# Block-sparse attention and a softplus FFN on one core: attention handed out in two pieces per unit instead of three, and TensorE in the program's own order

## The chip, the core and the metric

The kernel runs on one core of a Trainium2 chip. A core has five engines that work at the same time, each through its own queue in order: TensorE (PE; its weight loads are listed apart as PEld), VectorE (DVE), ScalarE (ACT), GpSimd (POOL) and SyncE (SP, which only issues DMAs here). The metric is the device time of one execution in microseconds (us). Matmul results land in PSUM, in eight banks; DMAs move data between HBM and the on-chip memory SBUF.

## The reference

Four batches of eight heads, 768 positions of 64 channels. A query block of 32 positions sees its neighbours, the first and the last block, and three sampled blocks; the first and the last query block see everything. The result, 3072 tokens of 512 channels, goes through one FFN with a softplus between its two matrices.

```python
scores = scale * np.matmul(q, k.transpose(0, 1, 3, 2))
mask = np.abs(blk_i - blk_j) <= window
mask = mask | (blk_i == 0) | (blk_j == 0) | (blk_i == n_blocks - 1) | (blk_j == n_blocks - 1)
for qb in range(n_blocks):
    for kb in sampled_blocks[qb]:
        mask[qb * block:(qb + 1) * block, kb * block:(kb + 1) * block] = True
...
attn = attn / (np.sum(attn, axis=-1, keepdims=True) + 1e-09)
x = np.matmul(attn, v)                      # then (tokens, heads * channels)
h = x @ w_in
g = np.maximum(h, 0.0) + np.log1p(np.exp(-np.abs(h)))
return g @ w_out
```

The weights come in 64 bit and are converted on the core; FFN operands are split into a high and a low part, so that each product takes three matmuls (high with high, high with low, low with high).

## The kernel before

**Attention.** A *set* is one group of four query blocks of a batch with all eight heads; each batch has six groups (the last with two blocks) and one *whole* set, the first and last query block against all 24 key blocks. That makes 28 sets. Each set has two *units* (a = 0 and 1, four heads each). A unit n goes through these steps, named by the tile that they write:

- `scores` (L581): 16 small matmuls into two PSUM tiles `s` (L601; `nc.tensor.matmul` on f32 stands twice in the trace, so 32 there), then VectorE's scaled and masked minimum, four instructions, out of `s` into `pr` (L607), which frees the `s` tiles. Whole sets: L625 and L632, four `s` tiles.
- `exponents` (L642): ScalarE, four activations on `pr` (L657).
- `transposes` (L661): eight TensorE transposes (L670) of `pr` into two PSUM tiles `t`, copied to `pt` by ScalarE (L677) and VectorE (L675).
- `values` (L682): 32 small matmuls (L700; 64 in the trace) of `pt` with the values `vg` into the PSUM tile `x` of the set, of which there is one buffer; whole sets L714.

When a set's two units are through, `normalise` divides (VectorE, L728 to L730, into `xs`), `turn` transposes `xs` on TensorE (L745, tile `y`), and `x_high` (ScalarE, L759) and `x_low` (VectorE, L763) write the two parts of the FFN's input `x`.

The tiles `s`, `t`, `y` and the FFN's hidden tile `h` all share four PSUM buffers (tag "s" of `ps_s`). A tile that takes a buffer must wait until the tile before it there was read.

**What feeds it.** Query, key, value and weight loads are issued by SyncE in the order of the program. Keys of a batch lie in one buffer `kT`; `gather_keys` copies the blocks of a set into `kg` (two buffers; sampled blocks by GpSimd, L511, ends by ScalarE, L480, the window by VectorE, L497). Values have two buffers `vg`: `load_values(m + 2)`, issued after the values matmuls of set m, brings the window and the ends, and GpSimd gathers the sampled blocks (L567). `gather()` (L460) takes one such GpSimd job of values and one of keys each time it is called. The next batch's keys are loaded after the scores of the whole set's second unit.

**FFN.** 128 steps of 384 tokens by 128 hidden columns, in two phases (48 and 80 steps). A step has 12 hidden matmuls (L237 to L239) and nine of the projection into three PSUM tiles `o` (L295 to L297), with softplus on ScalarE and VectorE between (L243 to L273). The weights of the first phase are converted while attention runs (`Weights.tick`, called through `convert`).

**Order.** `pieces(n)` (L768) makes three functions per unit: a score piece (`x_low`, then scores of unit n + 2, keys), a value piece (exponents of n + 2, `turn`, values of n, loads of values and queries) and a transpose piece (`x_high`, `normalise`, transposes of n + 1). `attend` (L862) runs the next piece, one `gather()` and one `convert()`. The first 22 pieces run alone; then the FFN starts, and `between(x)` (L898), called in the middle of the hidden matmuls, between the projection's three parts and at the half and end of a step, runs as many pieces as are due at that point: `due` (L888) spreads them evenly over the steps of the next 384 tokens. With three pieces per unit and about one step per unit, TensorE sees, over and over: scores, six hidden, three projections, values, six projections, transposes, six hidden.

SyncE's queue is in the order of the program. The other engines' queues, TensorE's among them, were ordered by the scheduler at build time, which in most places of TensorE's queue left the order of the program.

Of the kernel before, what the change touches and what calls it, by code (L numbers as in the profile page):

```python
# [32 lines left out]

FIRST = 11

START = 4

SPREAD = 2

# [11 lines left out]
def sparse_attention_ffn(  # L51
# [408 lines left out]
    def gather():  # L460
        for work in (value_work, key_work):
            if work:
                work.pop(0)[1]()
# [178 lines left out]
    def exponents(n):  # L642
        m, a = units[n]
        b, g, whole = sets[m]
        st = state[n]
        if a == 0:

            sums[m] = wk.tile([P, 2 * NP], F32, tag="sums", name=f"sums{n}", bufs=3)
        rs, nmax, rows = sums[m], st["nmax"], slice(0, st["rows"])
        for r in range(2):  # L650
            if whole:
                parts = [(st["pr"][r], 0, 2 * a + r)]
            else:
                w = NS * BLOCK
                parts = [(st["pr"][r][rows, j * w : (j + 1) * w], j, 2 * (2 * a + j) + r) for j in range(2)]
            for x, j, h in parts:
                nc.scalar.activation(  # L657
                    x, x, AF.Exp, bias=nmax[rows, r, j : j + 1], scale=-1.0, accum_out=rs[rows, h : h + 1]
                )
# [21 lines left out]

    def values(n):  # L682
        m, a = units[n]
        b, g, whole = sets[m]
        pt = state[n]["pt"]
        gathered(value_work, m)
        vd = vg[sets[m]]
        if a == 0:
            xps[m] = ps_x.tile([P, DM], F32, tag="x", name=f"x{n}")
        xq = xps[m]  # L690

        if not whole:
            ni = NI if g < NG - 1 else 2
            for j in range(2):
                for r in range(2):
                    h = 2 * (2 * a + j) + r
                    for c in range(2):
                        for i in range(ni):
                            rows = slice(i * BLOCK, (i + 1) * BLOCK)
                            nc.tensor.matmul(  # L700
                                xq[rows, h * D : (h + 1) * D],
                                pt[r, 2 * j + c][:, rows],
                                vd[:, c, i, h * D : (h + 1) * D],
                                start=(c == 0), stop=(c == 1),
                            )
        else:
            rows_v = vd.rearrange("p c i f -> p (c i) f")
            for r in range(2):
                at = (2 * a + r) * D
                for c in range(NCH):  # L710
                    for o in range(2):
                        rows = slice(64 * o, 64 * o + 64)
                        h = 2 * (2 * a + o) + r
                        nc.tensor.matmul(  # L714
                            xq[rows, at : at + D],
                            pt[r, c][:, rows],
                            rows_v[:, c, h * D : (h + 1) * D],
                            start=(c == 0), stop=(c == NCH - 1),
                        )
# [18 lines left out]
    def turn(m):  # L738

        b, g, whole = sets[m]  # L740
        xs = xss.pop(m)
        rows = P if whole or g < NG - 1 else 2 * BLOCK
        ps = ps_s.tile([P, NP, P], F32, tag="s", name=f"y{m}")
        for p in range(NA if whole else NP):
            nc.tensor.transpose(ps[:, p, 0:rows], xs[0:rows, p * P : (p + 1) * P], ident[0:rows, 0:rows])  # L745
        t, at = divmod(place[b, g], GROUPS)
        if (0, t) not in X:
            x_tile(0, t)
        if whole:
            hi, lo = (X[0, t][:, i, :, at * P + 64 : (at + 1) * P] for i in range(2))  # L750
            src = ps[:, 0:NA].rearrange("p a (o t) -> p (a o) t", o=2)
        else:
            hi, lo = (X[0, t][:, i, :, at * P : at * P + rows] for i in range(2))
            src = ps[:, :, 0:rows]
        turned[m] = (hi, lo, src)

    def x_high(m):
        hi, lo, src = turned[m]
        nc.scalar.copy(out=hi, in_=src)  # L759
# [8 lines left out]
    def pieces(n):  # L768

        ended = [units[i][0] if 0 <= i < len(units) and units[i][1] == NA - 1 else None for i in range(n - 2, n + 1)]  # L770

        scored = None
        if n + 2 < len(units) and units[n + 2][1] == NA - 1 and not sets[units[n + 2][0]][2]:
            scored = place[sets[units[n + 2][0]][:2]]

        def score_piece():
            if ended[0] is not None:
                x_low(ended[0])
            s = n + 2
            if s < len(units):  # L780
                scores(s)
                if scored is not None:
                    load_keys(scored + 2)
                m, a = units[s]
                b, g, whole = sets[m]
                if whole and a == NA - 1 and b + 1 < B:

                    gathered(key_work, place[b, g])
                    for n_ in range(4):
                        load_kT(b + 1, n_)  # L790
                    load_keys()

        def value_piece():
            if n + 2 < len(units):
                exponents(n + 2)
            if ended[1] is not None:
                turn(ended[1])
            if n < len(units):
                values(n)
                if ended[2] is not None:  # L800
                    load_values(ended[2] + 2)
            if scored is not None:
                load_queries(scored + 2)

        def transpose_piece():
            if ended[1] is not None:
                x_high(ended[1])
            if ended[2] is not None:
                normalise(ended[2])
            if n + 1 < len(units):  # L810
                transposes(n + 1)

        return score_piece, value_piece, transpose_piece

# [38 lines left out]
    spread_ends()  # L855
    attention = [piece for n in range(len(units) + 2) for piece in pieces(n)]

    needs = [3 * sum(1 for m, a in units if place[sets[m][:2]] < (t + 1) * GROUPS) + 4 for t in range(NTB)]
    needs[-1] = len(attention)
    done = 0  # L860

    def attend():  # L862
        nonlocal done
        attention[done]()
        done += 1
        gather()
        convert()

    SECOND = NTB * EARLY
    owed = 0.0  # L870

    def convert():

        nonlocal owed
        if done < START:
            return
        owed += EARLY_TICKS if weights.at < 4 * len(early) + 9 else LATE_TICKS
        while owed >= 1 and not weights.done():
            weights.tick()
            owed -= 1  # L880
            if weights.at == 4 * weights.extra + 2:
                extractx.close()
                pools["x2"] = ctx.enter_context(tc.tile_pool(name="x2", bufs=1))
# [97 lines left out]
```

## Time and profile before

| What | us |
|---|---|
| Median of three runs | 831.7 |
| Lowest and highest of the three | 827.58 and 833.89 |
| Span of the profiled execution, first to last instruction | 812.1 |
| TensorE busy in the span | 781.7 |
| VectorE, ScalarE, GpSimd busy | 574.8, 489.6, 223.3 |

The profile gives the span of the profiled execution, not its device time; the median of the runs is 19.6 us longer than that span.

A row of the timeline has start (us from the span's start), duration, engine, line, operation, tiles, shape and count; in brackets stands the time that the engine was idle before it and what ended that ("issue" when the profile shows nothing that it waited for). Matmuls overlap: what one costs on TensorE is the distance between two starts, not its duration. A row of the windows view has a stretch, its length, and for each engine the busy time in it with the number of instructions.

### The profile page before, as it was taken

Reading aid. Unit: us, or ns where it says so; the run is one execution under the profiler, and the core shown is the slowest. Engines: PE = TensorE matmul, PEld = TensorE weight load, DVE = VectorE, ACT = ScalarE, POOL = GpSimd, SP = SyncE. Lnnn points to the kernel's source line nnn. Section 1 sums busy time; section 2 is a strip of 40 time slices with the busy share of each in tenths; the row PEclk is TensorE's granted clock in tenths of the full one; section 3 lists DMA queues with packets and bytes.
Section 4 is the critical chain, followed back from the end, with each engine's and each line's share of the span. In section 5 each row is a group of like instructions: output and inputs, shape, how many; then the busy total and the mean of one; then the engine's idle time right before and its main releaser. Section 6 shows DMA issues by size and latency. Waiting matters only on the chain.

```text
span 812.1 us, 21433 instructions
## 1 busy us (share of the span) xinstructions
PE 781.7 (96%) x8108; PEld 647.6 (80%) x8108; DVE 574.8 (71%) x1474; ACT 489.6 (60%) x1182; POOL 223.3 (27%) x389
## 2 busy tenths in 40 slices
PE   8878898999999999999999999999999999999997
PEld 8545676877677777778778988999988999988996
DVE  5778999876887777886655985656565656656564
ACT  5878785757767767767565764444444444444442
POOL 6864775635565436563000000000000000000000
PEclk9999898999999999999999999999999999999999
DMA  8899678687696777866425640304040312122021
GB/s 254 241 257 336 171 212 266 195 294 247 184 291 198 248 261 200 267 171 184 158 78 182 250 178 20 137 1 155 2 146 10 116 40 105 52 88 68 0 79 40
DMA packets 48408, 129.65 MB, mean 160 GB/s; under 512 B 5489, under 2 KB 5617, under 8 KB 46257
## 3 DMA queue, kind: packets, MB, share of 16 engines
q1 hardware_dynamic: 42304, 109.79, 42.3%
q0 software_dynamic: 5712, 17.57, 7.6%
q8 instruction: 64, 1.05, 0.5%
q10 hardware_dynamic: 288, 0.93, 0.3%
q14 instruction: 40, 0.32, 0.1%
HBM read 97.85 MB, written 30.41 MB: 158 GB/s over the span
## 4 chain that ended last, share of the span: by engine, by line
PE 82%; DVE 7%; ACT 6%; DMA 2%; issue 2%; POOL 0%; SPq 0%; ACTq 0%; DVEq 0%; POOLq 0%
PE o L295 11%; PE h L237 11%; PE o L297 10%; PE o L296 10%; PE h L238 10%; PE h L239 10%; PE s L601 5%; PE t L670 4%; PE x L700 4%; ACT pr L657 3%; PE warm L831 2%; DMA kT<-in_k_dram 1%; PE s L625 1%; DVE pr L607 1%; PE x L714 1%
## 5 line engine op out<-in xcount | busy, mean ns | idle before, releaser
L237 PE MATMUL h<-x,w 128*128 128x384 f32 x512 | 180.0, 352 | 0.4 <-DVE nmax L632 0.2
L238 PE MATMUL h<-x,w 128*128 128x384 f32 x512 | 173.7, 339 | 0.0
L239 PE MATMUL h<-x,w 128*128 128x384 f32 x512 | 173.1, 338 | 0.0
L250 DVE TENSOR_SCALAR u<-e 128x384 f32<-128x384 f32 x128 | 50.8, 397 | 155.8 <-ACT e L244 154.4
L295 PE MATMUL o<-w,gh 128*128 128x512 f32 x384 | 158.7, 413 | 0.0
L657 ACT ACTIVATE pr<-pr,nmax 128x256 f32<-128x256 f32 (+2 forms) x208 | 110.4, 532 | 74.6 <-DVE nmax L607 60.4
L297 PE MATMUL o<-w,gl 128*128 128x512 f32 x384 | 152.0, 396 | 1.2 <-issue 1.0
L296 PE MATMUL o<-w,gh 128*128 128x512 f32 x384 | 151.7, 395 | 0.0
L243 ACT ACTIVATE e<-h 128x384 f32<-128x384 f32 x128 | 62.4, 487 | 114.9 <-PE h L239 114.8
L267 ACT CAST gh<-u 128x384 fp32r<-128x384 f32 x128 | 65.6, 513 | 79.2 <-PE o L296 78.1
L237 PEld LDWEIGHTS h<-x,w 128*128 128x128 f32 x512 | 96.6, 189 | 19.4 <-issue 11.2
L567 POOL DMA_INDIRECT vg<-in_v_dram,ix x88 | 90.3, 1027 | 65.9 <-PE x L700 39.1
L238 PEld LDWEIGHTS h<-x,w 128*128 128x128 f32 x512 | 96.8, 189 | 6.5 <-issue 2.2
L511 POOL COPY kg<-kT 128x128 f32 x252 | 86.0, 389 | 41.2 <-PE s L601 38.8
L239 PEld LDWEIGHTS h<-x,w 128*128 128x128 f32 x512 | 96.6, 189 | 0.0
L295 PEld LDWEIGHTS o<-w,gh 128*128 128x128 f32 x384 | 72.0, 188 | 19.9 <-issue 7.1
L297 PEld LDWEIGHTS o<-w,gl 128*128 128x128 f32 x384 | 72.1, 188 | 18.8 <-issue 1.5
L296 PEld LDWEIGHTS o<-w,gh 128*128 128x128 f32 x384 | 72.2, 188 | 10.3 <-issue 0.4
L607 DVE CUSTOM_DVE_ANT_1 pr<-s,mask 128x256 f32<-128x256 f32 (+1 forms) x192 | 69.6, 414 | 14.5 <-PE s L601 14.5
L258 ACT ACTIVATE u<-u 128x384 f32<-128x384 f32 x128 | 66.9, 523 | 15.4 <-DVE e L252 15.2
L263 DVE TENSOR_TENSOR u<-u,e 128x384 f32<-128x384 f32 x128 | 73.6, 575 | 3.0 <-ACT u L258 2.4
L273 DVE TENSOR_TENSOR gl<-u,gh 128x384 fp32r<-128x384 f32 x128 | 73.0, 570 | 2.8 <-ACT gh L267 2.8
(81 smaller groups left out, 1088.6 us busy)
## 6 DMA issues: line engine op xcount, KB each, us to landing
vg<-in_v_dram SPq DMA_DIRECT2D x19, 768.0 KB, 5.8
xD<-x SPq DMA_DIRECT2D x8, 1536.0 KB, 7.4
x<-xD SPq DMA_DIRECT2D x8, 1536.0 KB
raw<-in_w_in_dram SPq DMA_DIRECT2D x16, 512.0 KB, 9.3
raw<-in_w_out_dram SPq DMA_DIRECT2D x16, 512.0 KB, 8.3
qc<-in_q_dram SPq DMA_DIRECT2D x24, 256.0 KB, 6.9
vg<-in_v_dram SPq DMA_DIRECT2D x12, 512.0 KB, 7.4
yD<-os SPq DMA_DIRECT2D x24, 256.0 KB, 2.5
```

The lines of the kernel that those rows point to most:

```text
L237: nc.tensor.matmul(ph, wh[:, cols], hi[:, c], start=(c == 0), stop=False)
L238: nc.tensor.matmul(ph, wh[:, cols], lo[:, c], start=False, stop=False)
L239: nc.tensor.matmul(ph, wl[:, cols], hi[:, c], start=False, stop=(c == NC - 1))
L263: nc.vector.tensor_tensor(out=l, in0=l, in1=e, op=ALU.add)
L273: nc.vector.tensor_tensor(out=gl, in0=l, in1=G[n].bitcast(F32), op=ALU.subtract)
L295: nc.tensor.matmul(po[m], gh[:, cols], wh, start=first, stop=False)
L296: nc.tensor.matmul(po[m], gh[:, cols], wl, start=False, stop=False)
L297: nc.tensor.matmul(po[m], gl[:, cols], wh, start=False, stop=last)
L511: copy(out=kd[:, i, 1 + NR + s, :], in_=kT[b][:, bass.ds(x, 1), :].rearrange("p n f -> p (n f)"))
L567: nc.gpsimd.indirect_dma_start(out=vd[0 : 3 * BLOCK, 1, i, :], out_offset=None, in_=v, in_offset=bass.IndirectOffsetOnAxis(ap=ix[:, b, 4 * ...
L607: nc.vector.tensor_tensor_reduce(out=pr[r][rows, j], in0=ps[r][rows, j], in1=mask[rows, g].unsqueeze(2).to_broadcast([ni * BLOCK, NS, BLOCK]),
L657: nc.scalar.activation(x, x, AF.Exp, bias=nmax[rows, r, j : j + 1], scale=-1.0, accum_out=rs[rows, h : h + 1])
```

## The change

- `value_piece` is gone. Its exponents and `turn` move to the transpose piece, its values and loads to the end of the score piece. A unit has two pieces.
- `values(n)` of a set that isn't whole does nothing for its first unit, and for the second calls the new `products` for both units, one after the other. A whole set's units stay apart.
- `gather()` is called once after an odd piece and twice after an even one; `convert` counts each piece one and a half times. Per unit both stay as they were (three calls, three counts).
- START counts pieces: three instead of four. `needs`, the number of pieces after which 384 tokens are there, is two per unit plus three instead of three per unit plus four; the first FFN step follows 15 pieces instead of 22.
- TensorE's queue is in the order of the program, as SyncE's.

```diff
-START = 4
+START = 3
...
     def values(n):
         m, a = units[n]
+        whole = sets[m][2]
+        if a == NA - 1 and not whole:
+            for n_ in range(n - NA + 1, n + 1):
+                products(n_)
+        elif whole:
+            products(n)
+
+    def products(n):
+        m, a = units[n]
         b, g, whole = sets[m]
...
-        def value_piece():
-            if n + 2 < len(units):
-                exponents(n + 2)
-            if ended[1] is not None:
-                turn(ended[1])
             if n < len(units):
                 values(n)
                 if ended[2] is not None:
...
         def transpose_piece():
+            if n + 2 < len(units):
+                exponents(n + 2)
             if ended[1] is not None:
+                turn(ended[1])
                 x_high(ended[1])
...
-        return score_piece, value_piece, transpose_piece
+        return score_piece, transpose_piece
...
-    needs = [3 * sum(1 for m, a in units if place[sets[m][:2]] < (t + 1) * GROUPS) + 4 for t in range(NTB)]
+    needs = [2 * sum(1 for m, a in units if place[sets[m][:2]] < (t + 1) * GROUPS) + 3 for t in range(NTB)]
...
         gather()
-        convert()
+        if done % 2 == 0:
+            gather()
+        convert(1.5)
...
-        owed += EARLY_TICKS if weights.at < 4 * len(early) + 9 else LATE_TICKS
+        owed += share * EARLY_TICKS if weights.at < 4 * len(early) + 9 else share * LATE_TICKS
...
-    with _tile.TileContext(nc) as tc, tc.manual_schedule(engines={_mybir.EngineType.SP}):
+    with _tile.TileContext(nc) as tc, tc.manual_schedule(engines={_mybir.EngineType.SP, _mybir.EngineType.PE}):
```

What TensorE's queue looks like, as built, at two places of the stretch in which attention and FFN run side by side. A row is line, operation, tile written and tiles read, shape, and count. First, before: from the last projection matmul of a part, over `y` and the values of one unit, to the next two parts of the projection.

```order
L297 MATMUL o_0_3632<-w_2008,gl_3929 128x512
L745 MATMUL y_4080<-ident,xs_3990 128x128 x4
L700 MATMUL x_4086<-vg_174,pt_0_3995 32x64 x8
L700 MATMUL x_4086<-vg_174,pt_4_4002 32x64 x8
L700 MATMUL x_4086<-vg_174,pt_0_3995 32x64 x8
L700 MATMUL x_4086<-vg_174,pt_4_4002 32x64 x8
L295 MATMUL o_1_3654<-w_2008,gh_3861 128x512
L296 MATMUL o_1_3654<-w_2009,gh_3861 128x512
L297 MATMUL o_1_3654<-w_2008,gl_3929 128x512
L295 MATMUL o_2_3688<-w_2008,gh_3861 128x512
L296 MATMUL o_2_3688<-w_2009,gh_3861 128x512
L297 MATMUL o_2_3688<-w_2008,gl_3929 128x512
```

The transposes `t` come next. The values of a unit stand alone between matmuls of the FFN, and ten rows lie between `y` and `t`.

The same engine in the changed kernel, the values of a set (`x_4146`): from the last two scores matmuls to the next hidden ones.

```order
L601 MATMUL s_0_4124<-kg_178,qc_2_3699 32x256
L601 MATMUL s_1_4125<-kg_178,qc_2_3699 32x256
L709 MATMUL x_4146<-vg_174,pt_0_3983 32x64 x8
L709 MATMUL x_4146<-vg_174,pt_4_3990 32x64 x8
L709 MATMUL x_4146<-vg_174,pt_0_3983 32x64 x8
L709 MATMUL x_4146<-vg_174,pt_4_3990 32x64 x8
L709 MATMUL x_4146<-vg_174,pt_0_4089 32x64 x8
L709 MATMUL x_4146<-vg_174,pt_4_4096 32x64 x8
L709 MATMUL x_4146<-vg_174,pt_0_4089 32x64 x8
L709 MATMUL x_4146<-vg_174,pt_4_4096 32x64 x8
L237 MATMUL h_4113<-x_3_3121,w_1101 128x384
L238 MATMUL h_4113<-x_3_3121,w_1101 128x384
```

The values of both units now follow the scores of a set's second unit, with no FFN matmul between.

The other half of a set in the changed kernel: from the last scores matmul of a set's first unit to the transposes.

```order
L601 MATMUL s_1_4296<-kg_179,qc_3_3946 32x256
L237 MATMUL h_4285<-x_3_3121,w_1262 128x384
L238 MATMUL h_4285<-x_3_3121,w_1262 128x384
L239 MATMUL h_4285<-x_3_3121,w_1263 128x384
L237 MATMUL h_4285<-x_3_3121,w_1262 128x384
L238 MATMUL h_4285<-x_3_3121,w_1262 128x384
L239 MATMUL h_4285<-x_3_3121,w_1263 128x384
L295 MATMUL o_0_3633<-w_2264,gh_4110 128x512
L296 MATMUL o_0_3633<-w_2265,gh_4110 128x512
L297 MATMUL o_0_3633<-w_2264,gl_4232 128x512
L754 MATMUL y_4347<-ident,xs_4245 128x128 x4
L670 MATMUL t_0_4353<-ident,pr_0_4122 128x128 x4
```

Here `t` follows `y` at once; before, the values of a unit and six projection matmuls stood between. In the built programs of both kernels these two `t` tiles take the PSUM buffers of the two `s` tiles of the scores just ahead.

More of the change, by code (lines that the diff above doesn't have):

```diff
@@ L866, in attend, with convert @@
         gather()
-        convert()
+        if done % 2 == 0:
+            gather()
+        convert(1.5)
     SECOND = NTB * EARLY
     owed = 0.0
-    def convert():
+    def convert(share=1.0):
         nonlocal owed
```

## The prediction

> **What bounds the kernel now.** I read the page first, then the windows view cut where the character of the work changes, then TensorE's waits, then the timeline of one steady stretch.
>
> ```profile
> span 812.1 us, 21433 instructions
> PE 82%; DVE 7%; ACT 6%; DMA 2%; issue 2%; POOL 0%; SPq 0%; ACTq 0%; DVEq 0%; POOLq 0%
> 0.00:60.00 60.00, 48.67 (x949) 37.10 (x950) 41.27 (x155) 42.79 (x113) 44.41 (x95) 0.97 0.89 249
> 60.00:140.00 80.00, 69.85 (x995) 51.15 (x995) 75.05 (x187) 59.13 (x152) 50.73 (x73) 0.91 0.83 254
> 140.00:430.00 290.00, 285.27 (x4285) 219.49 (x4284) 217.75 (x643) 201.46 (x539) 128.17 (x221) 1.00 0.68 209
> 430.00:812.10 382.10, 377.94 (x1885) 339.89 (x1883) 240.71 (x492) 186.23 (x380) 0.00 (x0) 1.00 0.25 89
> ```
>
> The second row is the chain that ended last, by engine. The others are the windows, in the order TensorE, its weight loads, VectorE, ScalarE, GpSimd, granted clock, DMA share, GB/s. There are four stages. Up to 60 us attention runs alone, no engine is full, and the DMAs are (0.89). From 60 to 140 us the FFN starts while the first weights are converted: VectorE is busy 75.05 of 80 us, TensorE 69.85. From 140 to 430 us attention and FFN run side by side, and TensorE is busy 285.27 of 290. After 430 us only the FFN is left, on TensorE, and the change leaves that order alone. So TensorE time can be won in the third stage. In the second it is worth little, since VectorE's work is the same before and after, and the pace of conversion per unit too.
>
> **What the change removes.** In the third stage TensorE doesn't wait, but it loses time at each switch between the FFN's full matmuls and attention's small ones.
>
> ```profile
> 264.95 1.09 PE L601 MATMUL s<-kg,qc 64*32 64x256 f32 x32
> 265.98 0.45 PE L237 MATMUL h<-x,w 128*128 128x384 f32 x1
> 266.26 0.34 PE L238 MATMUL h<-x,w 128*128 128x384 f32 x1
> 266.44 0.34 PE L239 MATMUL h<-x,w 128*128 128x384 f32 x1
> 267.37 0.39 PE L296 MATMUL o<-w,gh 128*128 128x512 f32 x1
> 267.60 0.40 PE L297 MATMUL o<-w,gl 128*128 128x512 f32 x1
> 267.93 1.10 PE L700 MATMUL x<-vg,pt 128*32 128x64 f32 x64
> 268.96 0.50 PE L295 MATMUL o<-w,gh 128*128 128x512 f32 x1
> 269.30 0.40 PE L296 MATMUL o<-w,gh 128*128 128x512 f32 x1
> 19.96 1.10 PE L601 MATMUL s<-kg,qc 64*32 64x256 f32 x32
> 20.99 1.31 PE L700 MATMUL x<-vg,pt 128*32 128x64 f32 x64
> 140.00:430.00 290.00, 36.29 (x1920) 30.96 (x1920) 1.00 0.68 209
> 140.00:430.00 290.00, 9.71 (x288) 8.88 (x288) 1.00 0.68 209
> ```
>
> Two projection matmuls start 0.23 us apart (267.37, 267.60), but the last one before the values 0.33 (267.60, 267.93), and the first after them 0.34 before its successor (268.96, 269.30). A visit to the values costs 0.10 going in and 0.11 coming out, 0.21 us. Scores cost the same way: 0.28 instead of 0.18 between hidden matmuls after them. Where values stand right behind scores (19.96 and 20.99), scores take 1.03 us, just as they do ahead of hidden matmuls (264.95, 265.98), so a visit that is attached to the scores pays neither end: the exit that the scores paid is now paid by the values. The last two rows are the windows of L700 and L714, TensorE first: 1920 and 288 matmuls. Visits of 64, and of 32 in the groups of two blocks, and of 48 in whole sets (six each, two per batch in three batches) make 27 + 6 + 6 = 39. All but the last stand behind scores after the change: 38 x 0.21 = 8.0 us less. That is the gain, and it needs no other engine to be faster.
>
> A page of the Trainium skill speaks against part of it: TensorEngine Tiling (Array Packing), Key Properties, says that changing the tiling mode, not merely the tile, drains the engine, and scores (64x32 tiles) and values (128x32) are two modes. By that rule scores to values would cost a drain too, and the gain would be about three quarters, an estimate of 6 us. The row at 20.99 shows no such drain.
>
> A smaller gain: scores take the PSUM buffers of transposes just copied. Before, six hidden matmuls lie between; afterwards six projections too (1.4 us more).
>
> ```profile
> PE t L670 <- DVE x L763: 1.8, 1, 1.8
> PE s L601 <- ACT pt L677: 1.2, 2, 1.0
> PE o L297 <- issue: 1.0, 1, 1.0
> ```
>
> These are nearly all of TensorE's waits between 140 and 430 us. The second, 1.2 us, goes.
>
> **What the change adds.**
>
> *Transposes behind scores.* In the half set without values, the transposes follow the scores by 1.03 (scores) + 1.16 (six hidden, 0.28 and five of about 0.175) + 0.69 (three projections of 0.23) + 0.4 (`y`: 0.53 to the values below, 0.10 of it the switch) = 3.3 us; before, the values and six projections came between, 2.5 us more. They need the buffers of those scores, hence VectorE's four minimum instructions to be through.
>
> ```profile
> 258.58 0.60 PE L745 MATMUL y<-ident,xs 128*128 128x128 f32 x4
> 259.11 1.10 PE L700 MATMUL x<-vg,pt 128*32 128x64 f32 x64
> 255.70 1.09 PE L601 MATMUL s<-kg,qc 64*32 64x256 f32 x32
> 258.27 0.08 DVE L607 DVE_READ_ACCUMULATOR2_ANT nmax<- 128x1 f32 x1
> 333.14 1.19 PE L601 MATMUL s<-kg,qc 64*32 64x256 f32 x32
> 337.71 0.07 DVE L607 DVE_READ_ACCUMULATOR2_ANT nmax<- 128x1 f32 x1
> ```
>
> For the scores at 255.70 VectorE is through 2.65 us after the scores started, for those at 333.14 4.64 us. The second buffer is needed 0.4 us after the first, at 3.7. So a half set waits between nothing and 0.95 us. Half of 39 visits are about 19 sets: from 0 to 18 us. I take 0.2 us each, 3.8, nearer the first row, since VectorE is idle for a quarter of this stage (217.75 of 290 busy) and can be there early in most sets.
>
> *Instruction packets.* The waits put down to "issue" have a pattern.
>
> ```profile
> q8 instruction: 64, 1.05, 0.5%
> 41.42 1.08 PE L601 MATMUL s<-kg,qc 64*32 64x256 f32 x27 [0.93 <-issue]
> 49.85 0.64 PE L601 MATMUL s<-kg,qc 64*32 64x256 f32 x8 [2.11 <-issue]
> 261.89 0.50 PE L297 MATMUL o<-w,gl 128*128 128x512 f32 x1 [1.02 <-issue]
> 41.40:49.84 8.44, 5.30 (x127) 1.00 1.05 274
> 49.84:61.45 11.61, 9.91 (x253) 1.00 0.87 247
> 61.45:261.88 200.43, 187.45 (x2785) 0.97 0.79 241
> ```
>
> The instructions of a long queue come by DMA, 64 packets here for 8108 matmuls, about 127 matmuls with their loads each. Between one such wait and the next lie 127, 253 (two times 126.5) and 2785 (22 times 126.6) matmuls: whole packets. So TensorE then waited for a packet that was late while the DMAs were busy. Two values visits in a row are 128 matmuls in 2.06 us, a whole packet, where a packet lasts 8.6 us on average (4285 matmuls in 290 us). Bounds: nothing, if packets come early enough, and a wait of 1.02 us in each of 19 sets, 19 us. I take two more waits like that at 261.89, 2.0 us: where the packet's edges fall inside the stretch is a matter of count, and the double visit comes late in a set, when that set's loads have mostly landed.
>
> The Trainium skill puts this cost at next to nothing: Runtime: NRT & Kernel Launch, Instruction fetch mechanics, says that crossing a 16 KiB boundary is mostly hidden. By it the term is 0 and the sum 2 us lower; the three rows above disagree with it where the DMAs are full.
>
> *Batch changes.* The keys of the next batch can only load after the whole set's scores, and ScalarE's queue stands behind the copy of them.
>
> ```profile
> 187.28 1.81 PE s L625 x16
> 190.44 7.47 DMA kT<-in_k_dram
> 197.93 0.62 ACT kg L480
> 203.07 0.70 DVE x L763
> 203.82 0.66 PE t L670 x4
> ```
>
> From the scores (187.28) to the released transposes it is 16.5 us whatever TensorE does, and TensorE already waits 1.8 of them. It now gets there some 1 us sooner for each of two changes in this stage: 2.0 us of the gain are given back; bounds 0 and 4.
>
> *Moved at no cost.* Exponents and `turn` come one piece later; the transposes that need them still stand a unit away. The value loads on SyncE and GpSimd's gathers wait for the second values visit, as before; two or three weight loads on SyncE now stand behind a value load instead of ahead, and GpSimd's four gathers of a set stay together. In the third stage GpSimd is busy 128.17 of 290 us, which hides that. If values came late, the chain would show `vg` ahead of `x`. In the first stage I take nothing: 3.0 us of "issue" (two rows above) could go, or come a second time, since DMAs decide there.
>
> **The sum** on the span: -8.0 - 1.2 + 3.8 + 2.0 + 2.0 = -1.4, so 810.7. The median of the runs is 19.6 over the profiled span (831.7 against 812.1); with the same 19.6 it is 830.3 us.
>
> **The rivals.** About 1% is what a measurement of this kernel can tell from no change: faster means under 823.4, slower over 840.0.
>
> *A. The gain is spent on new waits* (the forecast, 830.3; by itself 823 to 838). For it: VectorE busy at 75%, ScalarE at 69%, with little room where the order gets tighter.
>
> *B. The gain stays.* VectorE gets to the scores in time, no packet is late, and the two waits of the first stage go too: 831.7 - 9.2 - 3.0 = 819.5. For it: one of the two quoted scores leaves room, and TensorE as good as never waits now. Against it: 3.3 us is too short for the other.
>
> *C. Packets decide, and it is slower.* The place is the double values visit behind the scores; the price 1.02 us in each of 19 sets, 19.4 us; with the rest of the sum (-3.4) that is 847.7, and from 12 late packets of that size on it is over 840.0. For it: DMA share 0.68 in the stage, and waits that are already there. Against it: only one in this stage before.
>
> *D. Transposes always wait as at 333.14*: 18 us instead of 3.8, so 844.5. Against it: a wait on TensorE gives VectorE time to catch up.
>
> *E. TensorE isn't faster by switching less*, because the scheduler's order of the other queues shifts: 831 to 835, inside A's range.
>
> **How the numbers follow.** A with E 0.57, B 0.25, C 0.11, D 0.07. The time is A's, 830.3. The range leaves out half of C and D and the low part of B: 818 to 843. Faster by over 1% is B, 0.25; slower is C and D, 0.18; the rest, 0.57, is within 1%.
>
> **What would show it.** Steps right: rows of L709 with 128 matmuls behind 32 of scores, and a step of 0.23 between all projections there; attention's end near 428 us; a wait of TensorE for VectorE's L607 at `t` of 3 to 4 us in the third stage. B: that wait is missing and the stage is 8 us shorter. C: "issue" ahead of `x` or of the first matmul behind it, over ten times. D: L607 ahead of `t` for over 10 us. Wrong altogether: the first two stages differ by more than 5 us, which I can't price from these rows, or VectorE's and ScalarE's orders differ so that the third stage is no longer TensorE's.

## The result and the profile after

The changed kernel takes 836.05 us (median of 18 runs, 831.93 to 841.76) beside 830.64 us for the one before (18 runs, 826.99 to 836.63): a ratio of 1.006, 95% interval 1.0039 to 1.008. That is within 1%, but slower, where the forecast was 830.3 and no loss. The runs that follow came from five chips, and these fall into two kinds: on chips 11, 6 and 7 the kernel before takes 809 to 811 us (kind B here, 'fast' in the expectations), on chips 14 and 2, and in this first comparison, 830 to 831 (kind A, 'slow'). On B the ratio is 1.0154 (1.0128 to 1.0181) in one comparison and 1.0201 (1.0162 to 1.024) in a second.

The first two profiles can't be laid side by side. That of before (span 812.1) is like those of kind B, that of after (span 834.8) like those of A. So both kernels were profiled again in one comparison (f1 and f2 below), on chip 7, of kind B, with spans of 810.9 and 825.0, and these are read here. First the chain that ended last, by engine, and three windows of the kernel before (TensorE, weight loads, VectorE, ScalarE, GpSimd, granted clock, DMA share, GB/s).

```profile
PE 81%; DVE 6%; ACT 5%; DMA 4%; issue 2%; SPq 0%; POOL 0%; POOLq 0%; ACTq 0%; DVEq 0%
0.00:60.00 60.00, 48.35 (x948) 37.15 (x949) 41.55 (x155) 42.71 (x113) 44.22 (x95) 0.97 0.89 248
60.00:140.00 80.00, 69.70 (x994) 50.99 (x994) 74.97 (x187) 59.01 (x152) 50.82 (x73) 0.91 0.84 253
140.00:430.00 290.00, 286.35 (x4292) 220.65 (x4291) 218.13 (x645) 202.51 (x541) 128.93 (x221) 1.00 0.68 209
```

The same of the changed kernel, with its span:

```profile
span 825.0 us, 21430 instructions
PE 71%; DVE 11%; ACT 9%; DMA 5%; issue 4%; SPq 1%; ACTq 0%; DVEq 0%
0.00:60.00 60.00, 47.07 (x850) 34.53 (x850) 39.80 (x151) 39.74 (x107) 42.29 (x94) 0.91 0.81 231
60.00:140.00 80.00, 64.36 (x1005) 47.91 (x1005) 71.38 (x178) 57.95 (x145) 49.77 (x74) 0.91 0.83 253
140.00:430.00 290.00, 271.59 (x4212) 214.28 (x4212) 223.21 (x634) 198.48 (x531) 130.35 (x223) 0.99 0.69 210
430.00:825.00 395.00, 390.74 (x2051) 351.24 (x2047) 247.96 (x513) 193.58 (x400) 0.00 (x0) 1.00 0.25 88
```

TensorE's share of the chain falls from 81% to 71%; VectorE's and ScalarE's grow by 5 and 4 points, issue doubles. In the third stage TensorE is busy 271.59 us of 290; before it was 286.35. The first stage has 850 matmuls in 60 us instead of 948: the loss begins there. The last attention tile `y` starts at 446.0 us instead of 432.0, and the rest, FFN alone, takes the same time in both. So all of it lies where attention runs: 7.3 us ahead of the first FFN matmul (66.5 us instead of 59.2), 6.7 behind it.

Now the larger of TensorE's waits over the whole span (engine, tile, line, what it waited for: us in total, times, longest), first before, then after, same chip.

```profile
PE t L670 <- DVE nmax L607: 5.0, 2, 2.8
PE x L700 <- ACT pt L677: 3.7, 2, 3.1
PE t L670 <- DVE x L763: 3.3, 2, 1.7
PE s L601 <- issue: 2.9, 2, 2.3
PE s L601 <- ACT pt L677: 2.3, 3, 1.9
PE o L297 <- issue: 1.0, 1, 1.0
```

```profile
PE t L670 <- DVE nmax L607: 10.4, 7, 3.9
PE x L709 <- issue: 5.8, 3, 2.3
PE s L601 <- ACT pt L677: 4.0, 4, 1.7
PE t L670 <- issue: 3.6, 2, 2.0
PE s L625 <- ACT pt L677: 2.8, 3, 1.5
PE x L723 <- ACT pt L677: 2.5, 2, 2.0
PE x L709 <- ACT pt L677: 2.1, 1, 2.1
PE s L601 <- issue: 1.9, 1, 1.9
```

Added up over all rows of that view, TensorE waits 25.1 us before and 45.7 after: 20.6 more, of which issue makes 7.0 (4.3 to 11.3), VectorE's minimum L607 6.0 (5.0 to 11.0), the `pt` copies 6.3 (6.7 to 13.0). The span grew by 14.1, so 6.5 us were gained on balance.

Behind the first FFN matmul the waits grow by 16.4 us and the time by 6.7, so some 9.7 are gained there. Ahead of it the waits grow by 4.2 and the time by 7.3: some 3 us are lost in another way, most likely to the clock. The granted clock up to the first FFN matmul is 0.92 instead of 0.97, and 0.74 instead of 0.93 from 30 to 40 us, where scores that otherwise take 1.03 us take 1.72 (33.70 to 35.42 in f2). The profiled execution of before, 813.0 us, is a long one beside its median of 809.0; by the medians the loss is 16.7 us.

Where nothing waits, the gain is plain. These are starts of the scores of one half of a set, first before, then after, in the last batch:

```profile
369.94 1.09 PE L601 MATMUL s<-kg,qc 64*32 64x256 f32 x32
385.44 1.09 PE L601 MATMUL s<-kg,qc 64*32 64x256 f32 x32
```

```profile
361.91 1.09 PE L601 MATMUL s<-kg,qc 64*32 64x256 f32 x32
376.90 1.09 PE L601 MATMUL s<-kg,qc 64*32 64x256 f32 x32
391.90 1.09 PE L601 MATMUL s<-kg,qc 64*32 64x256 f32 x32
```

A set takes 15.50 us before and 15.0 after, 0.5 less.

### The profile page after: what moved, and what is told of

Same layout as the page of the kernel before. It is cut to its first block, busy times and chain, and to the rows that moved or that the text cites. A ratio compares the mean times of both kernels' runs of the same rounds, so it can differ in the third digit from the quotient of the medians.

```text
span 834.8 us, 21430 instructions
## 1 busy us (share of the span) xinstructions
PE 776.3 (93%) x8108; PEld 646.7 (77%) x8108; DVE 583.6 (70%) x1474; ACT 489.1 (59%) x1182; POOL 225.7 (27%) x389
## 4 chain that ended last, share of the span: by engine, by line
PE 70%; DVE 13%; ACT 8%; issue 5%; DMA 3%; SPq 0%; another core or an unknown queue 0%; POOL 0%; ACTq 0%; DVEq 0%; POOLq 0%
PE h L237 10%; PE h L239 9%; PE o L295 9%; PE h L238 9%; PE o L297 9%; PE o L296 9%; ACT pr L657 4%; PE s L601 4%; PE x L709 3%; PE t L670 3%; DMA kT<-in_k_dram 2%; DVE pr L607 2%; PE warm L838 2%; ACT pt L677 2%; DVE wt L178 1%
## 5 line engine op out<-in xcount | busy, mean ns | idle before, releaser
L250 DVE TENSOR_SCALAR u<-e 128x384 f32<-128x384 f32 x128 | 48.1, 376 | 149.0 <-ACT e L244 147.3
L511 POOL COPY kg<-kT 128x128 f32 x252 | 91.6, 408 | 60.1 <-PE s L601 55.6
L567 POOL DMA_INDIRECT vg<-in_v_dram,ix x88 | 87.3, 993 | 55.6 <-PE x L709 30.0
L670 PE MATMUL t<-ident,pr 128*128 128x128 f32 (+1 forms) x480 | 65.3, 272 | 27.6 <-DVE nmax L607 17.6
L607 DVE CUSTOM_DVE_ANT_1 pr<-s,mask 128x256 f32<-128x256 f32 (+1 forms) x192 | 69.7, 416 | 26.3 <-PE s L601 11.4
L670 PEld LDWEIGHTS t<-ident,pr 128*128 128x128 f32 (+1 forms) x480 | 51.5, 141 | 40.5 <-issue 15.8
```

What stands on the lines that cost most here:

```text
L511: copy(out=kd[:, i, 1 + NR + s, :], in_=kT[b][:, bass.ds(x, 1), :].rearrange("p n f -> p (n f)"))
L567: nc.gpsimd.indirect_dma_start(out=vd[0 : 3 * BLOCK, 1, i, :], out_offset=None, in_=v, in_offset=bass.IndirectOffsetOnAxis(ap=ix[:, b, 4 * ...
L607: nc.vector.tensor_tensor_reduce(out=pr[r][rows, j], in0=ps[r][rows, j], in1=mask[rows, g].unsqueeze(2).to_broadcast([ni * BLOCK, NS, BLOCK]),
L670: nc.tensor.transpose(ps[:, i, 0:rows], st["pr"][r][0:rows, c * P : (c + 1) * P], ident[0:rows, 0:rows])
```

## The experiments

Three theories: *packets* (128 values matmuls in a row outrun the instruction packets), *distance* (scores, values, transposes and the next hidden tile stand too close for VectorE, ScalarE and the four shared PSUM buffers), *order* (TensorE's program order costs by itself). "Issue", "L607" and "pt" below are sums over all rows of TensorE's waits with that releaser. On B the runs from e1 to e4 come from chip 11, e5 to e8 from chip 6, f1 to f4 from chip 7; each ratio is to before on the same chip.

### Two kinds of chip: before and after again

Unchanged kernels.

> The kernel before once more, unchanged, for a second profile. The first profile of it spans 812.1 us, while the runs of it have a median of 830.64 (826.99 to 836.63); the profiled execution of the changed kernel spans 834.8 and its own time is 836.64, 1.8 us more. Theory: time is always about 1.8 us over the span, so the first profile of before was an uncommonly fast execution and a second one spans 825 to 833. Rival: some 19 us lie outside the span in before, and it spans 810 to 815 again. It leaves nothing out.

Measured: 807.87 us, span 805.7. The time is 1.8 to 2.2 us over the span in every profiled run, so nearly all of the 19.6 us between span and median that the forecast carried along were a difference of chips, not of span and time.

> The changed kernel once more, so that its profile comes from the same chip as those of the other experiments; nothing is left out. Theory 'chip': the 22 us between the runs of before in the first comparison (830.64) and in the second (808.83) are the chip's, so it takes 812 to 816 us where before takes 809, ratio 1.004 to 1.008, and its profile shows the first FFN matmul at 62 to 65 us instead of 69.43. Theory 'start': the 10 us that the first FFN matmul comes later are the change's, and it stands at 68 us or later here too.

Measured: 823.06 us, ratio 1.0154 (1.0128 to 1.0181). The chips do differ by some 20 us, but the loss is twice what 'chip' gave, and the first FFN matmul stands at 67.8 us (57.9 in e1): the late start is the change's. Then both kernels in one comparison.

> The kernel before, unchanged, for a profile beside the changed kernel's on one chip. So far the chips differ: before took 830.8 on one and 808.8 to 810.7 on another, and the profiles of before (spans 812.1 and 805.7) are of the fast kind, that of the changed kernel (834.8) of the slow kind. If this is a fast chip: span 804 to 812, waits of TensorE near 24 us. If a slow one: span 824 to 834, and its waits put down to L607 and pt well over the 2.2 and 8.8 us of the fast one.

> The changed kernel on the same chip as the three others; nothing is left out. Theory 'packets': on a fast chip ratio 1.012 to 1.018, waits put down to issue 10 to 13 us against 4 to 6 in before; on a slow one 1.004 to 1.008, issue 5 to 8, and the rest of the waits L607 and pt.

Measured: spans 810.9 and 825.0, ratio 1.0201 (1.0162 to 1.024), above what 'packets' gave; the waits as shown above, with 11.3 us of issue.

### One part of the change at a time

Program order alone, in before:

```diff
-tc.manual_schedule(engines={_mybir.EngineType.SP})
+tc.manual_schedule(engines={_mybir.EngineType.SP, _mybir.EngineType.PE})
```

> Before's three pieces with TensorE alone put in program order. Theory 'order' (program order by itself costs TensorE waits, since the scheduler's order had pulled waiting work apart): 834 to 839 us, ratio to before 1.004 to 1.010, most of it ahead of 140 us. Theory 'distance' (the tight distance from scores to transposes in the half set without values is what costs, and in three pieces values of a unit and six projections lie between): 828 to 832, ratio 0.997 to 1.002.

Measured: ratio 1.0034 (1.0011 to 1.0057), between the two, and its profile is as fast as that of before (805.3). A small cost at most.

The changed kernel without that line.

> The changed kernel with TensorE's order left to the scheduler. Theory 'order': the switching gain of 8 us stays and the waits go, 819 to 827 us, ratio 0.986 to 0.996. Theory 'distance': the scheduler moves transposes little, the waits for L607 stay near 15 us over the span, and the time stays at 833 to 838, ratio 1.003 to 1.009.

Measured: 1.006 (1.0035 to 1.0084), in the range of 'distance'. That is less than half of what the whole change loses on B (1.0154 and 1.0201, on other chips), but no gain appears.

The changed kernel with the values of each unit apart:

```diff
-        whole = sets[m][2]
-        if a == NA - 1 and not whole:
-            for n_ in range(n - NA + 1, n + 1):
-                products(n_)
-        elif whole:
-            products(n)
+        products(n)
```

> The changed kernel with the values of each unit behind the scores two units on, 64 matmuls a visit, instead of the set's 128 behind every second scores; still two pieces and program order, and still no visit that pays a switch of its own. So the switching gain is the same, and every scores has values (1.03 us) between it and the next transposes: 4.3 us from scores to transposes instead of 3.3 and 5.3. Theory 'distance': waits of t for L607 fall from 17.6 us to under 9 and the time to 824 to 831, ratio 0.992 to 1.001. Theory 'order' or 'start' (the FFN's first matmul comes 10 us later, 69.43 against 59.19): 833 to 838 as the changed kernel, ratio 1.003 to 1.009.

Measured: 1.0068 (1.0045 to 1.009). 'Distance' as stated falls: L607 is down to 5.6 us, but the time didn't follow, and pt is at 15.2. Against the whole change (1.0154, 1.0201, on other chips) about 1% is saved, and issue is 1.9 instead of 11 to 12.

Both taken away, so two pieces alone.

> The changed kernel with neither joint values nor program order: two pieces, the values of each unit behind the scores, TensorE's order left to the scheduler. Theory 'packets' (joint values are what costs): ratio 0.996 to 1.002, as the visits pay no switch and no packet holds more than 64 values matmuls and 32 of scores in a row. Theory 'distance' (two pieces alone cost, since scores, values, transposes and the next hidden tile stand closer on the four PSUM buffers): 1.004 to 1.008, as with program order (1.0068), and waits for pt over 12 us.

Measured: 1.0056 (1.0032 to 1.0079), 'distance': pt 13.0, issue 3.5.

Joint values alone, in before (the edit of `values` and `products` as in the change).

> Before with one part of the change: the values of a set's two units together, in the value piece of the second unit; three pieces and the scheduler's order stay. Half as many visits to the values, and each stands between projection matmuls, so some 19 visits less at 0.21 us: 4 us of switching gained. Theory 'packets': a packet that holds the 128 values matmuls has only some 20 full matmuls beside them, about 6 us instead of 8 to 9, so late packets cost 3 to 8 us more than in before, most of it ahead of 70 us, and the ratio is 0.999 to 1.006. Theory 'distance' or 'order' (joint values are innocent, the two pieces or the program order cost): the gain stays, ratio 0.993 to 0.997.

> Joint values alone again (three pieces, scheduler's order), beside the changed kernel on one chip. Theory 'joint values cost by themselves': ratio 1.008 to 1.015, so most of what the changed kernel loses. Theory 'they cost only on the slow chip': 0.998 to 1.004 if this chip is a fast one.

Measured: 1.0116 (1.0089 to 1.0144) on A, 1.0111 (1.0061 to 1.0161) on B. Both lie above every range that was given for e9: joint values cost by themselves. In f3 issue is 13.0 us, L607 and pt together only 7.2. But all its waits together are only 3.3 us more than in f1 (28.4 and 25.1), while its span is 5.2 longer and its median 10, although half of the visits to the values are saved. So the waits don't account for the whole loss of f3, and the rest stays open.

The sums of waits, in us, from the profiles on B, by part:

| Kernel | issue | L607 + pt |
|---|---|---|
| before (e1, f1) | 5.2, 4.3 | 11.0, 11.7 |
| before, program order (e2) | 3.8 | 10.0 |
| three pieces, joint (f3) | 13.0 | 7.2 |
| two pieces, per unit (e4, f4) | 1.9, 3.5 | 20.8, 18.0 |
| two pieces, joint, scheduler (e3) | 10.4 | 13.7 |
| the change (e5, f2) | 11.9, 11.3 | 20.1, 24.0 |

Joint values bring some 8 us of issue waits (means of 11.7 with, 3.7 without), two pieces 2 to 13 us of waits for L607 and pt, the least under the scheduler with joint values.

### Are the issue waits packets?

Rows of f2 with such waits, and windows between one and the next:

```profile
44.24 1.08 PE L601 MATMUL s<-kg,qc 64*32 64x256 f32 x27 [1.92 <-issue]
53.45 1.22 PE L709 MATMUL x<-vg,pt 128*32 128x64 f32 x73 [2.33 <-issue]
65.93 0.65 PE L709 MATMUL x<-vg,pt 128*32 128x64 f32 x32 [1.91 <-issue]
44.23:53.44 9.21, 6.70 (x126) 4.25 (x127) 7.83 (x26) 6.63 (x21) 7.54 (x11) 0.81 0.83 249
53.44:65.92 12.48, 8.08 (x253) 5.72 (x253) 8.57 (x28) 9.30 (x27) 5.70 (x6) 1.00 0.84 248
246.20:294.70 48.50, 46.76 (x760) 37.98 (x760) 38.78 (x108) 32.21 (x91) 23.26 (x34) 0.96 0.71 221
```

126, 253 and 760 matmuls are one, two and six packets, as in before. Some of these waits cost more than they last: the wait that ends at 246.2 is 1.97 us, and from there to 252.0 the granted clock is 0.71. To test it, the edges were moved:

```diff
-    for n in range(WARM):
+    for n in range(WARM - 40):
         nc.tensor.matmul(warm[:, n % 4], ident, ident, start=True, stop=True)
+    for n in range(80):
+        nc.tensor.matmul(warm[:, n % 4, 0:64], ident, ident[:, 0:64], start=True, stop=True)
```

> The changed kernel with 40 of the 50 warming matmuls at the start replaced by 80 of half their width: the same time, but 160 instructions more in TensorE's queue, so that every later packet edge of 256 instructions falls elsewhere. A set has about 2 x 256 instructions, so the edges keep their place in it through a whole batch; by the changed kernel's trace the edges now leave only 2.5 to 3 us, instead of 4.6 or more, for a packet that holds a double values visit. Theory 'packets': waits put down to issue grow from 5.9 to 15 us or more, and the time by 8 to 20 us over the changed kernel, ratio to before 1.016 to 1.03. Theory 'distance': the time stays, ratio 1.004 to 1.008, issue waits of 3 to 8 us.

Measured: 851.98 us, ratio 1.0513 (1.0483 to 1.0543), 29 us over the changed kernel in the same comparison; issue 24.4 us. The replaced matmuls don't take the same time, as the expectation has it: the first scores start at 23.4 us instead of 15.3 (e5), the first FFN matmul at 70.7 instead of 67.8. So at most 3 of the 29 us are lost ahead of the FFN. Its timeline, and the windows between:

```profile
139.74 0.43 PE L709 MATMUL x<-vg,pt 128*32 128x64 f32 x3 [4.63 <-issue]
156.16 1.98 PE L709 MATMUL x<-vg,pt 128*32 128x64 f32 x124
158.95 0.31 PE L709 MATMUL x<-vg,pt 128*32 128x64 f32 x4 [0.82 <-issue]
175.47 0.31 PE L709 MATMUL x<-vg,pt 128*32 128x64 f32 x5 [1.11 <-issue]
194.88 0.31 PE L709 MATMUL x<-vg,pt 128*32 128x64 f32 x5 [4.12 <-issue]
139.73:158.94 19.21, 17.86 (x253) 14.50 (x252) 13.71 (x37) 11.98 (x32) 7.68 (x12) 0.86 0.41 126
158.94:175.46 16.52, 15.40 (x253) 12.43 (x254) 12.74 (x38) 11.43 (x30) 9.52 (x18) 1.00 0.71 210
175.46:194.87 19.41, 15.29 (x254) 12.43 (x253) 13.52 (x38) 12.42 (x35) 6.17 (x6) 1.00 0.84 276
```

Set after set, here and again from 373 us on, the wait falls one to five matmuls ahead of the end of the 128, two packets after the last. Two packets are about one set, so an edge stays at its place in the set. Of the 29 us the waits put down to issue make only 12.5 (11.9 in e5, 24.4 here), those for L607 5.4. After the two longest shown here the granted clock falls, to 0.50 from 139.7 to 145.0 us and to 0.67 from 194.9 to 200.0; from 140 to 260 us it is 0.97 on average, where e5 has 1.00. The control is the same shift in before.

> A control for the shifted packet edges: before with the same replacement of 40 warming matmuls by 80 of half their width. Theory 'packets': in before no packet holds more than 64 values matmuls and 32 of scores without full matmuls between, so every position of the edges leaves 7 us or more in the stage with the FFN; the time moves by 1 to 3 us at most, ratio 1.000 to 1.005. Rival: the shift costs by itself (the start, the clock), ratio above 1.010, and then the 29 us of the same shift in the changed kernel aren't the double visit's.

Measured: 1.0049 (1.0026 to 1.0072), on A, where its first scores start late as well, at 24.1 us. On that kind of chip the shift by itself is no 29 us; on B the control wasn't run. So it is most likely the double visit that makes the edge's place decisive, and the changed kernel happens to have a better one.

### Distance

Transposes later:

```diff
-        while done < len(attention) and done < due(x):
+        while done < len(attention) and done < due(x - 0.2 * (done % 2)):
```

> The changed kernel with each transpose piece due a fifth of an FFN step later, which puts six projection matmuls instead of three between the scores' hidden half and the transposes, and the other three between the transposes and the next hidden half. From scores to transposes it is 4.0 us instead of 3.3 in the half set without values, and the next hidden tile no longer follows the transposes at once. Theory 'distance': the waits of t for L607 (17.6 us in the changed kernel's profile) and of h for the pt copies (3.7) fall to under 7 together, and the time to ratio 0.990 to 0.999 of before. Theory 'packets' (late instruction packets cost more): the waits for L607 fall, waits put down to issue stay or grow, ratio 1.000 to 1.005. Theory 'start': ratio 1.004 to 1.008, as nothing changes ahead of the first FFN matmul.

Measured: 1.0172 (1.0141 to 1.0204), above all three ranges; L607 went from 8.1 (e5) to 5.6, pt from 12.0 to 19.9. With the values per unit as well:

> Late transposes and the values of each unit behind the scores two units on (64 matmuls a visit, none with a switch of its own). From scores to transposes 4.6 to 5.0 us everywhere, packets never hold more than 64 values matmuls and 32 of scores in a row. Theory 'distance' and 'packets' alike: waits for L607 under 3 us, for issue under 3 us, and the switching gain shows: ratio 0.986 to 0.996. Theory 'start': the first FFN matmul still comes 3 to 4 us later than in before, ratio 0.997 to 1.004.

Measured: 1.008 (1.0054 to 1.0106), above both ranges; issue is at 4.8. Rows of the waits of e6, then of e8:

```profile
PE s L601 <- ACT pt L677: 7.7, 8, 2.3
PE x L709 <- issue: 7.1, 4, 2.6
PE t L670 <- DVE nmax L607: 5.0, 5, 1.6
```

```profile
PE s L601 <- ACT pt L677: 9.3, 8, 2.3
PE h L237 <- ACT pt L677: 3.7, 3, 2.1
PE t L670 <- DVE nmax L607: 0.5, 2, 0.3
```

The wait for L607 is gone in e8, and that for pt has taken its place (22.3 us in all): what is moved away from the scores ahead comes closer to the scores behind. With two pieces none of the orders tried has slack on the four buffers for `s`, `t`, `y` and `h`; more buffers were not tried.

### The start

```diff
-        if a == NA - 1 and not whole:
+        if n < 8:
+            products(n)
+        elif a == NA - 1 and not whole:
```

> The changed kernel, but the values of the first eight units (those ahead of the first FFN matmul) per unit, the rest joint. Theory 'packets in the start': the first FFN matmul comes at 61 to 63 us instead of 67.8, waits for issue ahead of 70 us fall from 8.4 to under 3 us, and the ratio from 1.015 to 1.006 to 1.010. Theory 'distance': the start stays at 66 us or later since the transposes still stand right behind the scores, ratio 1.013 to 1.018.

Measured: 1.0099 (1.0063 to 1.0135), on A, where the whole change has 1.006 (1.0039 to 1.008); first FFN matmul at 71.1 us (69.4 there). Inconclusive: the expectation was for B, and on A the start is late without the change too (see the end of the part on the prediction).

### A version to beat both

Three pieces and the scheduler's order for three batches; in the last, two pieces with values per unit, late transposes and program order.

```diff
+        if n >= SWITCH:                      # 42, the last batch
+            return (score_values, 1, 1.5, 0.0), (rest, 2, 1.5, LATE)
+        return tuple((f, 1, 1.0, 0.0) for f in (score_piece, value_piece, transpose_piece))
...
+        if done == 3 * SWITCH:
+            by_hand.enter_context(tc.manual_schedule(engines={mybir.EngineType.PE}))
```

> A version that may beat both: before, with its three pieces and the scheduler's order, for three batches; for the units of the last batch two pieces with the values of each unit (64 matmuls) behind the scores, transposes due a fifth of a step later, and TensorE in program order. In the profile with that arrangement throughout, the last batch took 99.0 and its end 8.3 us, where the second profile of before has 101.0 and 9.9. Theory 'packets' and 'distance' alike: 3.6 us gained, ratio 0.993 to 0.998, the last attention tile y 3 us earlier. Rival: the scheduler's part ahead shifts, or the waits come back, ratio 0.999 to 1.004.

> The version with three pieces for three batches and two for the last once more: in its first comparison it ran on a slow chip, where the values of the last batch waited for the sampled blocks' gathers (11.9 us of short waits at x), which no profile from a fast chip has. Theory 'the arrangement is better where nothing is late': on a fast chip the last batch and its end take 106 to 108 us instead of the 110.9 of before, ratio 0.994 to 0.999. Rival 'no gain in any case': ratio 1.000 to 1.004 with the last batch at 110 us or more. On a slow chip again: 1.002 to 1.006.

The third leaves the scheduler's order throughout and LATE at 0.

> The same split without program order and without the later transposes: three pieces for three batches, two pieces with the values of each unit for the last, TensorE's order the scheduler's throughout. In the profile of two pieces alone under the scheduler the last batch and its end took 99.9 and 7.6 us, against 101.0 and 9.9 in before on that chip. Theory 'switching gain where the loads are light': ratio 0.994 to 0.999 on a fast chip. Rival: the waits for pt and L607 in the last batch take it back, 1.000 to 1.004.

Measured, all on A: 1.0038 (1.0016 to 1.006), 1.0062 (1.0041 to 1.0082), 1.005 (1.0029 to 1.0071). None beats before: the first lies in the range of its rival, the other two a thousandth or less above the ranges given for no gain or a slow chip. On B it stayed untried.

## Why the prediction was wrong, step by step

The forecast was -1.4 us; the change costs 5 us on A, where it was measured first, and 12 to 17 on B. The gain came, but the costs were too small in the sum. In order of its terms, by f1 and f2 on B where nothing else is said:

- **The switching gain, 8.0 us** (0.21 a visit, two visits a set): right. 0.5 us a set where nothing waits, and some 9.7 us on balance behind the first FFN matmul, where part of the visits come ahead of the third stage. Nothing more is lost between scores and values: the scores take 1.03 us before values too (353.65 to 354.68 in f2), as ahead of hidden matmuls. By the Trainium skill, TensorEngine Tiling (Array Packing), Key Properties, a change of mode drains TensorE; a drain of its own between these two modes doesn't show in the trace.
- **"In the first stage I take nothing"**: this step failed on B. The first FFN matmul came at 66.5 us instead of 59.2, half of the loss. 7.7 us of waits for issue lie ahead of it, against 2.9, and the granted clock is lower. The prediction had said that the 3.0 us of issue there could come a second time, and left it at 0. Its sign of being wrong altogether, first stages that differ by more than 5 us, came true.
- **"Instruction packets ... I take two more waits like that at 261.89, 2.0 us"**: 7.0 us over the span. The reason given, that the double visit comes late in a set when loads have mostly landed, holds in the third stage (two waits, 3.6 us). But four of the six waits of f2 stand ahead of 66 us, the stage taken at nothing. The mechanism was named as rival C, at 1.02 us in each of 19 sets. f2 has six such waits of 1.6 to 2.3 us, three of them at the values; e7, with the edges moved, has nine at the values alone. The Trainium skill, Runtime: NRT & Kernel Launch, Instruction fetch mechanics, calls the crossing mostly hidden; here one crossing costs 2.35 us in before too (49.84 in f1), and up to 4.8 in e7.
- **"Transposes behind scores", 3.8 us**: right in kind, too small. L607 grew by 6.0 in f2. On A this is the step that failed most: 19.2 us in the changed kernel's first profile, against 1.0 to 4.8 in e10, e11, g1 and g2, the kernels nearest to before that have a profile there. That is rival D.

```profile
PE t L670 <- DVE nmax L607: 17.6, 14, 3.0
```

- **"A smaller gain: scores take the PSUM buffers of transposes just copied ... goes", -1.2 us**: wrong in sign, and behind the first FFN matmul the largest error on B. Waits for pt grew by 6.3 us over the span, by 7.2 there: at the whole sets' scores and values (L625, L723) and at scores, which two pieces bring closer to the transposes. On A the changed kernel has 17.1 us of them.
- **Batch changes, 2.0 us**: the place was right, the cause not as far as the rows show. The waits new at the whole sets, 5.3 us of the 6.3 just named, are for the pt copies and not for the next keys.
- **Time over span, 19.6 us**: wrong. It is about 2 us; nearly all the rest was another chip. It did no harm, as the forecast only carried it along.

So on B: 20.6 us of new waits, less 6.5 gained on balance, are the 14.1 on the span; the forecast had 7.8 of new costs against 9.2 gained. That the time on A is only 6 us over the forecast is luck: larger costs than forecast stand there, most likely, against a gain at the values that it hadn't named.

Why the loss is smaller on A (1.006) stays partly open. The profiles of kernels like before show many short waits there at the values, put down to issue, that the changed kernel hasn't; first e11, then the changed kernel's first profile:

```profile
PE x L703 <- issue: 11.9, 24, 1.2
```

```profile
PE x L709 <- issue: 0.4, 1, 0.4
```

In e11 they come several in one visit, some 0.7 us apart, so they are no packet edges; with the gathers of sampled blocks issued just ahead, late values are likely. The profiles from A show no landing times of these loads, so a wait for one would be put down to issue. Busy time and waits of the values matmuls together are 74.9 us in e10 and 78.5 in e11, but 60.9 in f1 on B; the changed kernel has 51.7 on A and 57.8 on B. So before most likely loses some 14 to 18 us at the values on A that the changed kernel, whose joint values come a unit later, doesn't lose. The late start isn't the change's alone there either: in e11, g1 and g2, which begin like before, the first FFN matmul comes at 64.0 to 68.8 us, in the changed kernel at 69.4. But before itself was never profiled on A, and joint values with three pieces (e9), which have only two waits at the values, lose 1.2% there; this wasn't tested further.

## What to carry to other kernels

A merge that saves switches also puts instructions closer together: count how many stand in a row against what an instruction packet holds (some 127 matmuls here), and what each shared PSUM buffer must have been through by then. Count it where the DMAs are fullest, not on average, and take no stage at nothing because it is short. And before two profiles are compared, make sure that they are from one chip.

## What was not expected of the hardware

- The place of the packet edges: 160 instructions more at the start cost 29 us (1.0513 beside 1.0154), at most 3 of them ahead of the FFN, and 0.5% in the kernel before.
- What a wait costs behind its end: after waits of TensorE of 4.63 and 4.12 us in e7 the granted clock is 0.50 and 0.67 for the next 5 us, after one of 1.97 us in f2 0.71. After one of 1.62 us (294.71 in f2) it stays at 1.00.
- Warming matmuls of half the width take far more than half the time: 160 of 128x64 take 17.9 us in e7 (5.48 to 23.39), 100 of 128x128 13.8 in e5 (1.46 to 15.30).
- Two kinds of chip: before takes 809 to 811 us on B (chips 11, 6 and 7) and 830 to 831 on A (14, 2 and the first comparison). No chip number stands in two comparisons, so a difference of the moment isn't ruled out.
